# A fused attention and Fourier-mixing kernel: a new order of all its steps, made with a price on changes of the PE array's shape

## The chip, the core and the metric

The kernel runs on one core of a Trainium2 chip. A core has five engines, each with its own in-order queue of instructions: PE (TensorE, matmuls; PEld in the profile is its weight load), DVE (VectorE), ACT (ScalarE), POOL (GpSimd) and SP (SyncE, which here only issues DMAs). The metric is device time in microseconds of one execution.

## The reference

Linear attention with exponential features (8 batches, 8 heads, 576 rows, 64 columns a head, 128 features), whose output goes through a two-dimensional Fourier transform and a two-layer network with a residual. Cut to what matters:

```python
def phi(x):
    proj = x @ w_phi
    proj = proj - max(abs(proj), axis=-1)
    return concatenate([exp(proj), exp(-proj)], axis=-1)
q_p, k_p = phi(q), phi(k)
num = q_p @ (k_p.T @ v)
den = q_p @ sum(k_p, over rows) + 1e-06
x = num / den                              # 8 x 576 x 512
u = x + real(fft(fft(x, axis=1), axis=2))
un = (u - mean(u)) / sqrt(var(u) + 1e-06)
out = u + relu(un @ w_ch1) @ w_ch2         # 512 -> 2048 -> 512
```

## The kernel before

All data of a batch stay on chip; the two network matrices W1b and W2b are loaded once, as bf16. The work of every batch is cut into generators, each with a letter, and each `next` of a generator is one step that emits some instructions:

- K, V, Q issue the loads of a batch's inputs on POOL's DMA queue (`load`, L284); B and A issue the DMA transposes on SP (L408 to L422); W issues the load of W1b (L93) in its first step and of W2b (L95) in its second.
- T makes the features: psk<-wphi,KT for keys and psh, ph for queries on PE, exponentials on ACT. P takes row maxima of the queries (psq on PE, MQ on DVE), R those of the keys (MK on DVE), S scales V by them (V4N, V4P, VCn, VCp on POOL).
- M runs the heads (kv at L887 and L891, pn at L987) and the Fourier stage (pm at L1021, psD at L1045, px at L1075, pu at L1104). D folds rows on DVE, N normalises (UN) and turns it to UT, U makes scales.
- F is the network of a batch: psf<-UT,W1b (L1224), relu to HT on ACT, pso<-W2b,HT (L1241, and L1267 for the last 64 rows).
- Y, C, H, Z, G, J occur in the opening alone: filling matmuls (idle, L1338), constants, sines, pads, and the PE transposes (pst, L368) of batch 0's keys (G) and queries (J).

Batch 0 is treated apart: its K, Q and V are loaded in f32 by SP, on the DMA queue q1 (`load_first`, L336), into space that belongs later to W2b and HT; they are turned on PE. The loads of POOL go through the DMA queue q0. SP's loads have the tiles' names W2b<-in_k_dram, W2b<-in_q_dram, HT<-in_v_dram.

The order of all steps is written out as a string of 1238 letters, `PLAN`; for each letter the kernel takes the next step of that generator. Nothing reorders the instructions afterwards: each engine's queue holds them as they were emitted. How the string came about is not part of the kernel.

A matmul is given a shape of the PE array (rows * columns): 128*128 for most; 64*128 where the contraction is over 64 (psk, psq, psh, ph), two of which use the two halves of the rows; 64*64 for the last 64 rows of keys and queries (L477, L527); 128*64 for the last 64 rows of the output (L1267).

```python
    with tc.manual_schedule():
        count_first()
        load_first()
        count_rest()
        for name in PLAN:
            step(name)
```

Of the kernel before, what the change touches and what calls it, by code (L numbers as in the profile page):

```python
# [20 lines left out]


PLAN = (
    "CCZCYYZYGGCTZVTRZKGTGRZWGJTTSJYRSJTQTTPPYTYRPTJMRJTMSMMSPSTKPTPTZMYTMMQTMTPMCQTMMTMTBDMHKMHKHDDHYAHY"
    "DYMYMHYTMMVMRTQMTNMMYTNTQNNYSFNMFNFNRVRFSTTPTFMFRSYUNTFWMURFVFFFFUUMTPMFBSTFMNTUTPNUSMFVPPCTFMFTUPQM"
    "TFMFTFPATVMFFFMMFTFMFKMFFMQFMFRTKFMFFRFPFDFFFFTFFFFTDFFFDRTFFFMFFTTDMFRFFFFSFFMFFFTFMSMFRFTMTTNMTFMN"
    "FPTMMFSSMTPMFTPPMTFFFMFFQNMPTFBSFMFFQMFFPTFFMNNUAMFFMFMFVTRTFFMFFVRVFFKMFKFFFFTMFMFFFFQMFPFDFFTPFRFF"
    "FTFDPFFTFFDDFFRFFTMFFFTMFFMMBSFFMSFRFTMMTFTNNFMFMMMKFTFMTSTFFFFSMPPTMTFFFFFMFSFMFPTMQQVFFFPTKFFMNNNM"
    "FFMFFMFFUMFFMFMFFFAMTRTVFFRTVFFFFFQMFFFDFDFTFFFDRFTPDFFFTPFFRFFTMFFFFTMMMFSFFRSFTMFTFMTTFNFTFMFNSMMM"
    "FMBSFKTTMQNFFFNPFMTFFFMFTPPFMFSFMNFPQMUTFVFKFPAFFMMFMFFVMFFMTFMFFMFFFMRTFRVFFTFFFQMFFFFTDDFRFFFFTFDP"  # L30
    "FFDFTPFFFRFTMTFFFFFMMMFFRFSFSTMSTFFMTFTFFNMFFTNMMMMSTTFMFFQNFTFPMFFFMFVNFMTBPPFSFMFFTPFMKFFFMFFQPNMF"
    "FMAUKFFMFFFMTTFRFRFMFFFTSFFFFVTMFFFRMTQFFFMTFFFFDFDFFFRFDFTFFDMFTFMFFMFSMFMRFTFFTMFTFTFFTMNNFPSMMMMV"
    "TFFSMTPMSTQFFMTPMFTFBQMFPPPFFMFFMFNVFPFFANNUMFFMFMTFMFFMFFMFFRTFRMFFFFFFFVTTPFSFFRFVFFMTFDFFTFFFDFDR"
    "FFFFFTDMTMFFFFFMMFFSFRFTMFTTTMNFMTNMFFFFMSFMMPSTFMFFFNFPTMFFFFFFMTPPSFMFFMFPTFMFFPNFFTMFNMFFMFMFFUFM"
    "FMFFFFMMFFFFFFMFFFFDFFFDFDFFFDFMFFMFFMFFMMFFMNMFFNFFFFFFMFMFMFFFFFFFFFFFFFFFFFFFNFFFFFNFNFFFUFFFFFFF"
    "FFFFFFFFFFFFFFFFFFFFFFFFFFFFFFFFFFFFFF"
)

# [1368 lines left out]
```

## Time and profile before

| what | value |
|---|---|
| median of 3 runs | 426.52 us |
| the 3 runs | 426.52, 426.04, 428.52 us |
| span of the profiled execution, first to last instruction | 423.1 us |
| its granted TensorE clock | 0.999 |
| DMA: packets, bytes, mean rate | 108761, 42.70 MB, 101 GB/s |

The time of the profiled execution itself is not recorded apart from its span; the median of the runs is 3.4 us above that span. The profile gives, for each engine, the busy time and the number of instructions; the chain of work that ended last, followed back; what each engine waited for; and time lines. A time line merges equal instructions that follow each other (x12) into one row, with its start, its length and, in brackets, the idle time of the engine before it and what ended it. Matmuls overlap, so the distance of two starts tells more than a length.

### The profile page before, as it was taken

What the parts mean: (1) busy time and instruction counts of PE and PEld (TensorE: products, weight loads), DVE (VectorE), ACT (ScalarE), POOL (GpSimd) and SP (SyncE); (2) the same over time, 40 slices, a digit from 0 to 9 for tenths busy, and PEclk for the clock granted to TensorE, in tenths of its full rate; (3) what the DMA queues carried; (4) which work ended last, traced back from release to release, by engine and by line L of the source; (5) the groups of instructions that cost most, each with busy time, mean ns of one, the idle gap of its engine ahead of it and who ended that gap; (6) DMA issues with size and microseconds to landing.
All of it is one profiled execution on the core that took longest, in us unless ns stands there. A gap on an engine that the chain in (4) does not pass through costs nothing.

```text
span 423.1 us, 10390 instructions
## 1 busy us (share of the span) xinstructions
PE 397.4 (94%) x4093; PEld 256.1 (61%) x4122; DVE 331.1 (78%) x681; ACT 306.3 (72%) x626; POOL 207.8 (49%) x271
## 2 busy tenths in 40 slices
PE   8787798999899999999999999999999999999995
PEld 3454475744676558655675558665766567656563
DVE  4989788798979976998779885898989786968103
ACT  6978799748975899489847898588868887353460
POOL 7982688525646077706673282834755331500000
PEclk9999999999999999999999999999999999999999
DMA  8999959984569468853899069954895081103313
GB/s 218 206 165 163 148 88 174 145 83 76 89 102 180 72 101 106 123 84 49 112 153 138 2 91 136 131 71 66 117 138 77 14 102 32 27 0 72 72 26 87
DMA packets 108761, 42.70 MB, mean 101 GB/s; under 512 B 82857, under 2 KB 103721, under 8 KB 108713
## 3 DMA queue, kind: packets, MB, share of 16 engines
q0 software_dynamic: 45936, 16.60, 37.1%
q1 hardware_dynamic: 62215, 24.85, 34.8%
q8 instruction: 32, 0.52, 0.5%
q10 hardware_dynamic: 562, 0.59, 0.5%
q14 instruction: 16, 0.13, 0.1%
HBM read 36.77 MB, written 9.44 MB: 109 GB/s over the span
## 4 chain that ended last, share of the span: by engine, by line
PE 61%; DVE 20%; ACT 8%; POOL 5%; DMA 2%; issue 2%; DVEq 0%; ACTq 0%; POOLq 0%
PE psf L1224 21%; PE pso L1241 19%; DVE R L903 3%; PE kv L887 3%; DVE cb L999 3%; DVE tg L994 2%; PE pso L1267 2%; PE psD L1045 2%; DMA UT<-UN 2%; PE pu L1104 2%; PE psq L547 1%; DVE MK L511 1%; PE psk L491 1%; PE psh L597 1%; DVE X L1094 1%
## 5 line engine op out<-in xcount | busy, mean ns | idle before, releaser
L1224 PE MATMUL psf<-UT,W1b 128*128 128x320 bf16 (+1 forms) x1024 | 142.5, 286 | 2.4 <-DMA UT<-UN 1.5
L1241 PE MATMUL pso<-W2b,HT 128*128 128x512 bf16 x467 | 117.1, 379 | 1.7 <-issue 0.5
L1224 PEld LDWEIGHTS <-W1b 128*128 128x128 bf16 x1024 | 94.0, 98 | 29.7 <-issue 4.3
L1229 ACT ACTIVATE HT<-psf 128x320 bf16<-128x320 f32 x128 | 53.5, 442 | 27.0 <-PE psf L1224 21.6
L1241 PEld LDWEIGHTS <-HT 128*128 128x128 bf16 x496 | 44.8, 98 | 44.6 <-issue 2.6
L1002 POOL TENSOR_TENSOR X<-cb,rd 128x320 f32<-128x320 f32 x56 | 41.5, 746 | 38.6 <-DVE rd L1001 37.3
L466 POOL TENSOR_TENSOR VCn<-VS,VCn 128x512 bf16<-128x512 bf16 x28 | 29.7, 1061 | 38.1 <-ACT VCn L461 35.3
L1231 ACT ACTIVATE HT<-psf 128x512 bf16<-128x512 f32 x64 | 37.9, 605 | 12.6 <-PE psf L1224 12.0
L555 DVE TENSOR_REDUCE MQ<-psq 128x8 f32<-128x1024 f32 (+1 forms) x32 | 34.3, 1084 | 13.4 <-PE psq L547 13.2
L1247 DVE SCALAR_TENSOR_TENSOR X<-pso,rs,X 128x512 f32<-128x512 f32 x31 | 22.8, 735 | 21.6 <-PE pso L1241 21.6
L497 ACT ACTIVATE KPn<-psk 128x1024 bf16<-128x1024 f32 x28 | 28.6, 1021 | 14.0 <-DVE MK L511 13.9
L497 ACT ACTIVATE KPp<-psk 128x1024 bf16<-128x1024 f32 x28 | 28.7, 1025 | 11.1 <-PE psk L491 11.1
L451 POOL TENSOR_TENSOR V4N<-VS,V4N 64x256 bf16<-64x256 bf16 x14 | 8.7, 623 | 53.9 <-ACT V4N L447 53.4
L511 DVE TENSOR_REDUCE MK<-psk 128x8 f32<-128x1024 f32 x28 | 33.9, 1212 | 1.0 <-ACT KPp L497 0.7
L1094 DVE TENSOR_TENSOR X<-pu,X 128x512 f32<-128x512 f32 (+3 forms) x49 | 23.3, 526 | 11.2 <-PE pu L1104 8.9
L466 POOL TENSOR_TENSOR VCp<-VS,VCp 128x512 bf16<-128x512 bf16 x28 | 29.7, 1059 | 0.0
L606 ACT ACTIVATE QPHP<-psh 128x1024 bf16<-128x1024 f32 x28 | 28.9, 1031 | 0.8 <-PE psh L597 0.6
L606 ACT ACTIVATE QPHN<-psh 128x1024 bf16<-128x1024 f32 x28 | 29.0, 1035 | 0.0
L1150 ACT ACTIVATE UN<-X,MV 128x512 bf16<-128x512 f32 (+1 forms) x35 | 24.5, 723 | 5.4 <-DVE MV L1175 3.1
L1174 DVE BATCH_NORM_STATS2 st<-X 128x6 f32<-128x512 f32 (+1 forms) x40 | 27.1, 677 | 0.3
L1190 POOL TENSOR_TENSOR rs<-VE,mhalf 128x5 f32<-128x5 f32 (+1 forms) x9 | 10.3, 1145 | 29.0 <-DVE VE L1189 29.0
L987 PEld LDWEIGHTS <-QPHP 128*128 128x128 bf16 x280 | 21.2, 99 | 4.6 <-DVE cb L999 1.0
(465 smaller groups left out, 825.0 us busy)
## 6 DMA issues: line engine op xcount, KB each, us to landing
out_dram<-X SPq DMA_DIRECT2D x15, 256.0 KB
out_dram<-X SPq DMA_DIRECT2D x60, 64.0 KB
QS<-in_q_dram POOLq DMA_DIRECT2D x14, 256.0 KB, 6.2
KS<-in_k_dram POOLq DMA_DIRECT2D x7, 512.0 KB, 7.4
VS<-in_v_dram POOLq DMA_DIRECT2D x14, 256.0 KB, 5.1
W1b<-in_moe_w_ch_dram POOLq DMA_DIRECT2D x1, 2048.0 KB, 13.1
W2b<-in_moe_w_ch_dram POOLq DMA_DIRECT2D x1, 2048.0 KB, 14.8
W2b<-in_k_dram SPq DMA_DIRECT2D x2, 512.0 KB
```

Of the source, the lines that this page charges most:

```text
L466: nc.gpsimd.tensor_tensor(out=VC[:, hs, :, 0:D], in0=values[b][0][:, hs, :].rearrange("p h (j d) -> p h j d", d=D), in1=VC[:, hs, :, D:D + ...
L497: nc.scalar.activation(out=KP[:, hs, :, :].rearrange("p e (jp jj) f -> p jj (e jp) f", jj=2), in_=psk[:], func=AT.Exp, scale=sgn,)
L511: nc.vector.tensor_reduce(out=MK[:, 2 * pr:2 * pr + 2, :].rearrange("p e (jp jj) -> p jj (e jp)", jj=2), in_=tiles[pr][:], axis=AX.X, op=A ...
L555: nc.vector.tensor_reduce(out=o, in_=i[:], axis=AX.X, op=ALU.max, apply_absolute_value=True)
L606: nc.scalar.activation(out=o, in_=psh[:], func=AT.Exp, scale=sgn)
L1002: nc.gpsimd.tensor_tensor(out=X[:, :, D * h:D * h + D], in0=cb[:, :, 0:D], in1=rd[:].to_broadcast([128, 5, D]), op=ALU.mult,)
L1094: nc.vector.tensor_tensor(out=to, in0=more, in1=to, op=ALU.add)
L1174: nc.vector.bn_stats(out=st[0:M, :], in_=X[0:M, c, 0:C])
L1224: nc.tensor.matmul(ps, lhsT=W1b[:, cc, 128 * hh:128 * hh + 128], rhs=UT[:, cc, lo:hi], start=(cc == 0), stop=(cc == NCC - 1),)
L1229: nc.scalar.activation(out=HT[:, hh, lo:hi], in_=ps, func=AT.Relu, scale=-1.0)
L1231: nc.scalar.activation(out=HT[:, hh - 1:hh + 1, lo:hi], in_=psw[:].rearrange("p (a n) -> p a n", a=2), func=AT.Relu, scale=-1.0,)
L1241: nc.tensor.matmul(po[:], lhsT=HT[:, hh, at:at + 128], rhs=W2b[:, hh, :], start=(hh == 0), stop=(hh == NHH - 1),)
```

## The change

Only the string `PLAN` differs. Every step, and with it every instruction, is the same, 4108 matmuls and all DMAs among them; they stand in another order, in whose making a change of the PE array's shape between successive matmuls was given a price. The first line of 13, of which 12 differ:

```diff
 PLAN = (
-    "CCZCYYZYGGCTZVTRZKGTGRZWGJTTSJYRSJTQTTPPYTYRPTJMRJTMSMMSPSTKPTPTZMYTMMQTMTPMCQTMMTMTBDMHKMHKHDDHYAHY"
+    "WYYYCCGCZZCGTGTGRJTRTTGZJYZSJRTSTPPRYTPYTJRJTSKMMSMTYPMPSTKTPTMMVTMMTTPMMMCTBTMDTHHMMQDHZYYHDDZQYQVA"
...
 )
```

On PE, successive matmuls differ in shape at 205 places before and at 194 now. Taken by stretches: ahead of batch 0's pm 30 and 33, from there to the end 175 and 161. Ahead of the first psf (L1224) stand 472 matmuls before and 500 now; the added ones are 16 psk, 8 psq and 4 pu, while ahead of batch 0's pm there are 400 before and 412 now (4 idle and 8 of L477 more).

POOL in the opening, before. The rows are in the order of its queue: constants, pads, loads into VS, KS and QS for batch 1, the load of W1b, and the multiplications by V of batch 0:

```order
L139 IOTA gs 128x128
L197 TENSOR_SCALAR gs<-ga,pn 128x320 x3
L268 MEMSET QPHP 128x8x64
...
L271 MEMSET V4P 128x520
L284 DMA VS_249<-in_v_dram 64x4x64 x2
L271 MEMSET V4N 128x520
L284 DMA KS_265<-in_k_dram 64x8x64
L274 MEMSET HI_105 128x512
L274 MEMSET HI_106 128x512
L93 DMA W1b<-in_moe_w_ch_dram 128x4x2048
L852 TENSOR_TENSOR V4N<-HT,V4N 64x4x64 x2
```

The same queue now:

```order
L139 IOTA gs 128x128
L93 DMA W1b<-in_moe_w_ch_dram 128x4x2048
L197 TENSOR_SCALAR gs<-ga,pn 128x320 x3
L268 MEMSET QPHP 128x8x64
...
L271 MEMSET V4P 128x520
L271 MEMSET V4N 128x520
L852 TENSOR_TENSOR V4N<-HT,V4N 64x4x64 x2
```

The load of W1b moved ahead of everything that POOL waits for, and the loads of batch 1 moved behind the first multiplications by V.

DVE in the opening, before (L375 copies a transpose of keys, KT, or queries, QT, from PE's results; L838 and L833 are the maxima of the keys; QT_172 is the first piece of Q):

```order
L833 TENSOR_REDUCE MK_180<-ps_236 128x4
L375 CAST KT<-pst 128x512 x2
L838 TENSOR_REDUCE MK<-psk 128x2x4
L375 CAST KT<-pst 128x512
L375 CAST QT_172<-pst 128x2x256
```

And now:

```order
L375 CAST KT<-pst 128x512 x2
L833 TENSOR_REDUCE MK_180<-ps_237 128x4
L375 CAST QT_172<-pst 128x2x256
L838 TENSOR_REDUCE MK<-psk 128x2x4
L375 CAST KT<-pst 128x512
```

The copy of the first piece of Q moved ahead of the maxima of the first pair of heads and of a copy of keys.

PE in batch 3, before (L576 projects the last 64 rows of the queries in shape 64*128, L597 the others; kv is 128*128):

```order
L891 LDWEIGHTS K4n
L891 MATMUL kv<-V4N,K4n 128x65
L576 LDWEIGHTS wphi_97
L576 MATMUL ph_2808<-QT_2211,wphi_97 128x256
...
L1267 LDWEIGHTS HT
L1267 MATMUL pso<-W2b,HT 64x512
```

And now:

```order
L891 LDWEIGHTS K4n
L891 MATMUL kv<-V4N,K4n 128x65
L597 LDWEIGHTS wphi_97
L597 MATMUL psh<-QT_2160,wphi_97 128x512
...
L576 LDWEIGHTS wphi_97
L576 MATMUL ph_2798<-QT_2161,wphi_97 128x256
...
L1241 LDWEIGHTS HT
L1241 MATMUL pso<-W2b,HT 128x512
```

L597 and L576, which have the same shape, stand next to each other now, where L576 stood alone between two other shapes.

More of the change, by code (lines that the diff above doesn't have):

```diff
@@ L23 @@
 PLAN = (
-    "CCZCYYZYGGCTZVTRZKGTGRZWGJTTSJYRSJTQTTPPYTYRPTJMRJTMSMMSPSTKPTPTZMYTMMQTMTPMCQTMMTMTBDMHKMHKHDDHYAHY"
[L25 to L33, printed above, removed]
@@ L34 @@
-    "FFFFFTDMTMFFFFFMMFFSFRFTMFTTTMNFMTNMFFFFMSFMMPSTFMFFFNFPTMFFFFFFMTPPSFMFFMFPTFMFFPNFFTMFNMFFMFMFFUFM"
-    "FMFFFFMMFFFFFFMFFFFDFFFDFDFFFDFMFFMFFMFFMMFFMNMFFNFFFFFFMFMFMFFFFFFFFFFFFFFFFFFFNFFFFFNFNFFFUFFFFFFF"
+    "WYYYCCGCZZCGTGTGRJTRTTGZJYZSJRTSTPPRYTPYTJRJTSKMMSMTYPMPSTKTPTMMVTMMTTPMMMCTBTMDTHHMMQDHZYYHDDZQYQVA"
+    "YVTMMHTMMRTPHSMTTVRMNMMTYQYKNYTNRNSNQMMTFNFTUSNFFFRYFRNMKNWFFMFUUUSTPQMUFTFMTPBFMFFNPCSTFFMTPFMTPUMT"
+    "FFUPTTFAFMFTMFMQFMFMFFMFFPTDFFMRFFFFMFFFRFFKFTDFFTTQDTFDFFFFRFRSVFFFTSMFFMVFTFFFFMMTFSFFMRFSFTMTFMTF"
@@ new lines @@
+    "FNNKPMMMMTMTPMFPQMTPTMFFFFBFNFFSMFTPKMFAFFPTFMNNFMFFMMFUFMTFRTFFFFFRFTMFFMFFMFFMFFTPFQFFQRFFTDFFFTDP"
+    "FFFFDFKDPFFVRMFFTVFFTMVFBFMMKTFSFFMSSFFQTRMFSTFMPNNFMMMFFMTTTFMFFFFTPMTFFFMFFNMFFSVMNFPTMFFAFPTFMNUM"
+    "FFMFMFFFMFFFMMFFFVFFMFTTDFFMFTFFTFFKFRTRFFDFDPRFFDSFFQFVTPFFFFRMMFTTVFTBFFFFSMMFFRFMFTTTMNFTMNMFFMFS"
+    "FMFFMTTMFQFNNQFFSPSMTFFFMFFPTPMFTFMFNFPMAFUFMFPMFMFFMFFVMFFMTTRFQTFMRQFFFSFFFMMFFFTFFDFFFFFRFTFKFDDP"
+    "FFDFTPFRFFFMFFTTFMTFFMFSMFRFSFMFTTTMFFFNFFTMNVKMMMFMFSTTMFFNNFFPMTFSPFFMFFMTPFMFFQMFNPTFBFFPAFFUMMFM"
@@ L36 @@
+    "FFFMTTFMRFKFFVTFFFRMFFQVFFFMTFTFFMFFFMRFFFFFFFTFDFDFFVDFFDFRMFFTTMTFFKMFSMSRFFMFTTTMNMMTNFSFFSFVFFPM"
+    "MMTFFMBTPMFTFMSTPFMTFFMFNPQPPMQFFMFFPNMFFMFFNAFMFMFFFMFUFMTVTFRFTRFFMFFFFFSFPTFFTFFMFFFVFFTFFDFDRFFF"
+    "DRFDFFTTMTMFFFFFFMMSRFFFMFTTTMFNFMMTFSNMFFMFMFSTPFFFFPTMFFFTMNPFNFPPMFFFMFFMFNSFPTFMFTFMFFFMFUMFMFFF"
+    "FMFMFFFMFMFFFFMFFFFFDFFDFDFDFFFMMFFFFMFMFMFFFMNMFNFFFFFMFFMFMFFNFFFFFFFFFFNFFNFFFFFFFFFFUFFFFFFFFFFF"
     "FFFFFFFFFFFFFFFFFFFFFFFFFFFFFFFFFFFFFF"
```

## The prediction

> **What bounds the kernel now.** I read the page first, its busy times and its chain by engine; then the busy time by stretch; then what PE waited for; then single rows of the opening. From the page:
>
> ```profile
> span 423.1 us, 10390 instructions
> PE 397.4 (94%) x4093; PEld 256.1 (61%) x4122; DVE 331.1 (78%) x681; ACT 306.3 (72%) x626; POOL 207.8 (49%) x271
> PE 61%; DVE 20%; ACT 8%; POOL 5%; DMA 2%; issue 2%; DVEq 0%; ACTq 0%; POOLq 0%
> ```
>
> PE is busy 94% of the span and carries 61% of the chain. But the share is a mean over unlike stages, so the span is cut at the matmul pm of batch 0 (41.7 us) and at 80 us (columns: the stretch, its length, then the busy time of PE, PEld, DVE, ACT and POOL with their instructions, the granted clock, the DMA share and GB/s):
>
> ```profile
> 0.00:41.70 41.70, 32.78 (x400) 19.73 (x401) 33.44 (x74) 33.11 (x62) 30.21 (x53) 1.00 1.06 189
> 41.70:80.00 38.30, 32.97 (x403) 22.87 (x403) 30.04 (x75) 34.74 (x74) 27.22 (x36) 1.00 1.12 138
> 80.00:423.10 343.10, 331.64 (x3296) 213.45 (x3321) 267.63 (x534) 238.48 (x492) 150.34 (x183) 1.00 0.65 86
> ```
>
> From 80 us on PE is busy 331.6 of 343.1 us. Before that, nothing is full but the DMA engines (share 1.06 and 1.12); four engines hand work to each other. What PE waited for from 80 us on is little (the largest rows and the smallest; in the view of waits each has total, times and the longest):
>
> ```profile
> PE psf L1224 <- DMA UT<-UN: 1.5, 2, 1.0
> PE ph L576 <- DVE MQ L555: 0.8, 1, 0.8
> PE psf L1224 <- ACT HT L1229: 0.7, 2, 0.3
> ...
> PE psk L491 <- DVE cb L999: 0.2, 1, 0.2
> ```
>
> Its eight rows add up to some 4.6 us. So the last 343 us can gain only what PE itself has less to do, and any delay of the opening goes through to the end.
>
> **The price of a change of shape.** The time line of PE (start, time, instruction; overlapping pieces, so starts are compared):
>
> ```profile
> 201.21 0.19 PE L891 MATMUL kv<-V4P,K4p 128*128 128x65 bf16 x1
> 201.24 0.29 PE L887 MATMUL kv<-VCn,KPn 128*128 128x65 bf16 x4
> 201.37 0.19 PE L891 MATMUL kv<-V4N,K4n 128*128 128x65 bf16 x1
> 201.49 1.49 PE L1267 MATMUL pso<-W2b,HT 128*64 128x512 bf16 x12
> ```
>
> Behind the same matmul L891 the next one of the same shape starts 0.03 us later, and one of shape 128*64 starts 0.12 us later. Nothing is waited for, so the change of shape itself costs 0.09 us. In the order of the instructions PE changes its shape 205 times before and 194 times now; ahead of pm of batch 0 it is 30 and 33, behind it 175 and 161. Behind pm 14 fewer at 0.09 us are worth 1.3 us. Ahead of it the 3 more (0.3 us) lie where PE waits for others, and cost nothing as long as it does.
>
> The Trainium skill, "TensorEngine Tiling (Array Packing)", section Tiling Modes, says that changing the mode, not merely the tile, drains TensorE; the 0.09 us agree. Its page "TensorE: Matmul & The Clock Gate", section Single matmul latency, gives a constant of 166 ns for a matmul that hides no drain; by that figure the same 14 would be an estimated 2.3 us. The row is of this kernel and decides.
>
> **The moved weight load.** The new table begins with W, the step that issues the load of W1b. Before, POOL came to it at 15.7 us (POOL's time line):
>
> ```profile
> 2.92 0.24 POOL L139 IOTA gs<- 128x128 f32 x1
> 4.39 1.57 POOL L197 TENSOR_SCALAR gs<-ga,pn 128x320 f32<-128x320 f32 x3 [1.23 <-DVE pn L192]
> ...
> 15.71 0.79 POOL L93 DMA_DIRECT2D W1b<-in_moe_w_ch_dram  x1
> ```
>
> Now it stands right behind that IOTA, so it is issued at 3.2 us, in a hole of 1.23 us: its 0.79 us on POOL cost nothing. Its transfer is another thing. From 2 to 16 us the DMA engines are full with the first K, Q and V, which SP issues into queue q1. Three windows of the DMA view (queue, packets, MB, share of 16 engines): 5 to 7 us, while K and Q arrive alone; 21 to 26 us, W1b beside a transpose of SP; 76 to 78 us, loads of POOL beside a transpose:
>
> ```profile
> q1 hardware_dynamic: 641, 0.48, 100.0%
> ...
> q0 software_dynamic: 241, 0.99, 97.1%
> q1 hardware_dynamic: 225, 0.06, 8.7%
> ...
> q0 software_dynamic: 572, 0.17, 82.1%
> q1 hardware_dynamic: 571, 0.15, 65.0%
> ```
>
> Two queues that both have work get one packet each in turn, whatever their size: 241 to 225, 572 to 571. W1b's packets carry 4 KB (0.99 MB in 241), so its 2 MB are 512 of them, at 48 per us 10.7 us. While they run, q1 gets through about 512 packets, for which alone it needs 512 / 320 = 1.6 us (641 in 2 us). So everything that q1 holds behind the second piece of K arrives 10.7 - 1.6 = 9.1 us later. That this load was hidden before is due to the transfers ahead of it having ended; that cover is gone. Late next are Q, then V. PE says when Q was needed:
>
> ```profile
> 11.25 0.66 PE L368 MATMUL pst<-ident,W2b 128*128 128x128 f32 x4 [1.06 <-DVE KT L375]
> 12.66 0.63 PE L368 MATMUL pst<-ident,W2b 128*128 128x128 f32 x4 [0.43 <-DMA W2b<-in_q_dram]
> 41.72 0.38 PE L1021 MATMUL pm<-HI,ones_b 128*128 128x512 bf16 x1 [1.81 <-ACT HI L917]
> 53.59 1.04 PE L1224 MATMUL psf<-UT,W1b 128*128 128x256 bf16 x8
> ```
>
> The transposes of the second piece of Q, at 12.66, waited for its DMA, so there was no slack: they go to 21.7 us. What of these 9.1 us reaches pm? From there DVE and ACT are the fuller engines:
>
> ```profile
> 12.30:24.00 11.70, 8.37 (x96) 4.99 (x97) 10.88 (x13) 11.02 (x22) 11.36 (x16) 1.00 1.02 206
> 24.00:31.70 7.70, 7.11 (x129) 5.03 (x129) 6.19 (x13) 5.52 (x17) 6.30 (x9) 1.00 0.94 151
> 31.70:41.70 10.00, 7.74 (x121) 5.03 (x118) 9.40 (x24) 8.03 (x13) 2.42 (x4) 1.00 1.43 164
> ```
>
> DVE works 26.5 of these 29.4 us, so a crowded restart can win back at most 2.9 us; half of that, 1.5, since it waits for PE and ACT, which are as late. DVE has one copy of Q (0.68 us, row below) more behind it at that point than before. That gives pm 9.1 - 1.5 - 0.7 = 6.9 us later; the ends are 9.1 (nothing won back) and 5.5 (all of it).
>
> ```profile
> 13.47 0.68 DVE L375 CAST QT<-pst 128x512 bf16<-128x512 f32 x1
> 14.25 1.23 DVE L838 TENSOR_REDUCE MK<-psk 128x8 f32<-128x1024 f32 x1
> ```
>
> The order would even let DVE lose there: the MK reduction of the first pair (1.23 us), which could run while nothing arrives, now stands behind that copy of Q. This leans to the upper end. The later loads of batch 1, which POOL now issues behind its multiplications, slip with the opening and are not waited for sooner.
>
> **Other work ahead of the first psf.** In the new order 28 matmuls more stand ahead of the first psf of batch 0: 16 psk, 8 psq and 4 pu. At 53.59 us PE had the first psf behind waits:
>
> ```profile
> 46.86 0.54 PE L1075 MATMUL px<-CS,CEO 128*128 128x289 bf16 x3
> 47.74 0.40 PE L491 MATMUL psk<-wphi,KT 64*128 64x128 bf16 x8 [0.35 <-ACT ET L1057]
> 56.88 0.39 PE L547 MATMUL psq<-wphi,QT 64*128 64x128 bf16 x8
> ```
>
> At 0.40 us for eight psk or psq, and as much for the four pu, this is 1.6 us that PE can do in its holes there. The gain lies between 0 (their inputs are late too) and 1.6; I take 1.0, as the holes are there but the keys come from the same late loads.
>
> **The rest of the order.** From pm of batch 1 on the links of each batch (pm, psD, pu, psf) lie within about 2 us of PE work of where they lay. I price that at nothing, with +-1 us: the 4.6 us of waits can shift, but there is little to win or lose.
>
> **Sum.** 6.9 - 1.3 - 1.0 = +4.6 us on the profiled span of 423.1 gives 427.7. The runs have a median of 426.5, 3.4 us above the span; the same 3.4 on top gives 431.1 us. With the ends, 5.5 - 1.3 - 1.6 - 1 = +1.6 and 9.1 - 1.3 + 1 = +8.8: 428.1 to 435.3.
>
> **Rivals.**
> - *The load passes unnoticed.* If q1 kept most of the engines' time while W1b ran, or Q had slack, only the 1.3 us of changes of shape remain: 425.2 us. The even packets speak against it, and the wait at 12.66. For it speaks that q1 there held one transpose at a time, never a deep backlog as in the opening.
> - *Faster.* POOL loses four things ahead of its first multiplication by V (two loads of V, one of K, the issue of W1b, the memsets of HI). If inputs were in time, kv would no longer wait for it (2.1 us in the waits, row below). With 1.3 and 1.6 that makes 421.5 us. It decides only if V lands by about 16 us, as before; by the packets it lands near 25.
>
> ```profile
> PE kv L887 <- POOL VCp L869: 2.1, 3, 1.3
> 16.51 1.34 POOL L852 TENSOR_TENSOR V4N<-HT,V4N 64x256 bf16<-64x256 f32 x2
> ```
>
> - *Nothing is won back and a new wait comes.* The upper end, 9.1 us at pm, with batch 1's loads (behind the late multiplications on POOL) late as well, by the 1 us of the last POOL item: 436 us.
>
> **How the numbers follow.** The forecast gets 0.70, the unnoticed load 0.17, faster 0.07, the last 0.06. The likeliest is 431.1 us. A range of 424.8 to 435.3 takes in the forecast's own 428.1 to 435.3 and the unnoticed load at 425.2, and leaves out about 0.15. About 1% (4.3 us) is what a measurement of this kernel can tell from no change: under 422.3 is faster, over 430.8 slower. The forecast lies at that border: 0.6 of its 0.70 is above it, with the last rival 0.48 slower. Faster is 0.06, since part of that rival stays within 1%. The rest, 0.46, is the same.
>
> **What would show it.** W1b's issue near 3.2 us on POOL, and 4 KB packets between 5 and 16 us. The transposes of Q at 20 to 22 us, waiting for the DMA of Q; V4N on POOL at 22 us or later; pm of batch 0 at 47 to 51 us instead of 41.7; from pm on to the end 1 to 4 us less than the 381.4 us of before. I am wrong if Q's transposes stand near 12.7 us (queues do not share so), or if pm is late but the time is not (the later stages had slack that the waits do not show), or if waits of psf for UT grow beyond 1.5 us.

## The result and the profile after

The changed kernel takes 451.3 us (median of 4 runs, 450.05 to 455.71), the kernel before 426.28 us beside it: a ratio of 1.061 (1.055 to 1.067). It is 25 us slower. I had forecast 431.1 us and a range up to 435.3.

The page of the changed kernel, first its span, its busy times, the granted clock by slices and the chain by engine:

```profile
span 449.4 us, 10389 instructions
PE 405.8 (90%) x4093; PEld 261.5 (58%) x4122; DVE 329.8 (73%) x681; ACT 306.3 (68%) x626; POOL 208.7 (46%) x271
...
PEclk9599769979999999999999996999999999999998
...
PE 64%; DVE 14%; DMA 11%; ACT 6%; issue 2%; POOL 1%; SPq 0%; DVEq 0%; POOLq 0%; ACTq 0%
```

The span grew by 26.3 us. PE does the same matmuls and is busy 8.4 us longer (405.8 against 397.4), and idle for the other 17.9 us. DMA has 11% of the chain, where it had 2%. The clock line has digits below 9 in five places; before, it was 9 in every slice (mean 0.999).

The stretches of the changed kernel, cut at the same work as before (pm of batch 0 starts at 48.9 us now), and below them four that are cut where the granted clock changes. The columns are those of the windows in the prediction:

```profile
0.00:48.90 48.90, 35.40 (x412) 21.46 (x413) 30.01 (x74) 33.23 (x63) 33.45 (x60) 0.90 0.87 151
48.90:87.20 38.30, 32.94 (x337) 21.31 (x338) 27.84 (x67) 31.87 (x66) 20.64 (x25) 0.82 0.92 114
...
13.40:23.60 10.20, 3.47 (x21) 2.91 (x22) 2.34 (x3) 1.80 (x2) 0.00 (x0) 0.50 1.10 244
50.90:64.50 13.60, 10.14 (x60) 5.13 (x61) 9.27 (x23) 8.39 (x18) 5.37 (x8) 0.50 0.94 106
95.30:102.10 6.80, 4.40 (x37) 2.81 (x38) 3.34 (x6) 1.90 (x3) 3.12 (x4) 0.50 0.54 63
272.80:279.60 6.80, 3.02 (x21) 2.27 (x22) 0.44 (x1) 0.60 (x1) 1.68 (x3) 0.50 1.08 123
```

In the second stretch PE starts 337 matmuls in 38.3 us; in the same length after its pm the kernel before started 403. In the last four the granted clock is 0.50: PE runs at half speed.

What PE waits for, ahead of 41 us (first row) and from there on:

```profile
PE pst L368 <- DMA W2b<-in_q_dram: 10.4, 1, 10.4
...
PE psf L1224 <- DMA UT<-UN: 8.8, 3, 5.7
PE psq L547 <- DMA QT<-QS: 5.1, 2, 2.7
PE psk L491 <- DVE cb L999: 3.5, 4, 2.4
```

So there is one long wait in the opening, for Q, and then single waits of 2 to 6 us in the later stages, for transposes by DMA (QT, UT) above all, and for DVE. Put against the same work in the trace of before, the delay grows in steps (the 65th psf of a batch stands for the middle of its network):

| work | before, us | now, us | delay | forecast of the delay |
|---|---|---|---|---|
| pm of batch 0 | 41.7 | 48.9 | +7.2 | +6.9 |
| first psf of batch 0 | 53.6 | 67.4 | +13.8 | +5.9 |
| 65th psf of batch 0 | 69.9 | 80.8 | +10.9 | |
| pm of batch 1 | 93.5 | 112.0 | +18.5 | |
| pm of batch 4 | 235.7 | 255.0 | +19.4 | |
| 65th psf of batch 4 | 272.4 | 299.2 | +26.8 | |
| end | 423.1 | 449.4 | +26.3 | +4.6 |

The first row is as forecast. The rest is not: three jumps, of 6.6 us between pm and the first psf of batch 0, of 7.6 us by pm of batch 1, and of 7.4 us in batch 4.

**The first jump.** PE's time line of the changed kernel:

```profile
20.13 1.09 PE L368 MATMUL pst<-ident,W2b 128*128 128x128 f32 x4 [10.37 <-DMA W2b<-in_q_dram]
...
48.90 0.39 PE L1021 MATMUL pm<-HI,ones_b 128*128 128x512 bf16 x1 [0.44 <-ACT HI L917]
51.13 0.61 PE L491 MATMUL psk<-wphi,KT 64*128 64x128 bf16 x8 [1.84 <-DVE CEO L1034]
...
55.96 0.61 PE L547 MATMUL psq<-wphi,QT 64*128 64x128 bf16 x8 [2.66 <-DMA QT<-QS]
56.50 1.63 PE L1045 MATMUL psD<-CS,CEO 128*128 128x289 bf16 x6
57.92 0.93 PE L1075 MATMUL px<-CS,CEO 128*128 128x289 bf16 x3
```

The eight psq of batch 1, which stood behind the first psf before (at 56.88), now stand ahead of the last psD and of px. PE takes its work in order, so the Fourier stage of batch 0 waits behind them for QT of batch 1. And all of it runs at half clock: three px take 0.93 us here and took 0.54 before. Of the 6.6 us, 4.4 are longer busy time of PE (from pm to the first psf 13.44 us for 88 matmuls, at a mean granted clock of 0.63, against 9.06 for 72); the rest is idle time. QT is late since its transposes are. SP's time line, the first transpose of these queries, before:

```profile
39.52 1.25 SPq L420 DMA_TRANSPOSE QT<-QS  x1
```

and now:

```profile
47.73 4.71 SPq L420 DMA_TRANSPOSE QT<-QS  x1
```

It takes 4.7 us instead of 1.25. The DMA view (queue, packets, MB, share of 16 engines) shows what runs beside it. From 39 to 44 us in the kernel before:

```profile
q1 hardware_dynamic: 3710, 0.92, 90.0%
q0 software_dynamic: 36, 0.02, 5.2%
```

and from 47 to 56 us in the changed one:

```profile
q1 hardware_dynamic: 3573, 0.89, 76.8%
q0 software_dynamic: 1086, 0.53, 73.5%
```

About as many packets of q1 needed 9 us instead of 5; POOL's loads of K, V and Q, issued between 36 and 45 us, run beside them.

**The second jump.** Between the middle of batch 0's network and pm of batch 1, PE waits twice, first for QT of batch 2 and then for DVE:

```profile
95.35 0.61 PE L547 MATMUL psq<-wphi,QT 64*128 64x128 bf16 x8 [2.40 <-DMA QT<-QS]
98.31 0.61 PE L491 MATMUL psk<-wphi,KT 64*128 64x128 bf16 x8 [2.35 <-DVE cb L999]
```

With the half clock from 95.3 to 102.1 us PE is also busy 3.2 us longer there (26.18 against 22.99, for 259 matmuls against 251), so waits and clock make up the 7.6 us.

**The last jump.** In batch 4, POOL (first two rows) issues a load of V and one of K, 768 KB, as SP begins the transposes of UT that psf needs:

```profile
264.11 0.81 POOL L284 DMA_DIRECT2D VS<-in_v_dram  x1
264.91 0.90 POOL L284 DMA_DIRECT2D KS<-in_k_dram  x1
...
266.80 2.81 SPq L1167 DMA_TRANSPOSE UT<-UN  x2
...
270.57 3.82 SPq L1167 DMA_TRANSPOSE UT<-UN  x2
...
276.58 2.74 PE L1224 MATMUL psf<-UT,W1b 128*128 128x256 bf16 x12 [5.69 <-DMA UT<-UN]
```

The DMA view of 265 to 272 us:

```profile
q0 software_dynamic: 1530, 0.77, 88.7%
q1 hardware_dynamic: 449, 0.36, 23.2%
```

The load gets 1530 packets through and the transposes with the stores 449. The wait is 5.7 us, and the twelve psf behind it take 2.74 us at half clock. In the kernel before the same twelve, at 252.41 us, took 1.48 us and had waited 0.47 us.

### The profile page after: what moved, and what is told of

It reads as the page before. It is cut to its first block, busy times and chain, and to the rows that moved or that the text cites. A ratio compares the mean times of both kernels' runs of the same rounds, so it can differ in the third digit from the quotient of the medians.

```text
span 449.4 us, 10389 instructions
## 1 busy us (share of the span) xinstructions
PE 405.8 (90%) x4093; PEld 261.5 (58%) x4122; DVE 329.8 (73%) x681; ACT 306.3 (68%) x626; POOL 208.7 (46%) x271
## 4 chain that ended last, share of the span: by engine, by line
PE 64%; DVE 14%; DMA 11%; ACT 6%; issue 2%; POOL 1%; SPq 0%; DVEq 0%; POOLq 0%; ACTq 0%
PE psf L1224 23%; PE pso L1241 17%; DMA W2b<-in_q_dram 4%; DMA QT<-QS 4%; PE kv L887 3%; DMA UT<-UN 3%; DVE cb L999 3%; PE psD L1045 3%; DVE tg L994 2%; PE psk L491 2%; PE pu L1104 2%; PE pso L1267 2%; DVE R L903 2%; PE psq L547 1%; PE idle L1338 1%
## 5 line engine op out<-in xcount | busy, mean ns | idle before, releaser
L1224 PE MATMUL psf<-UT,W1b 128*128 128x320 bf16 (+1 forms) x1024 | 144.4, 289 | 9.5 <-DMA UT<-UN 8.8
L1224 PEld LDWEIGHTS <-W1b 128*128 128x128 bf16 x1024 | 95.4, 99 | 37.7 <-DMA UT<-UN 9.1
L1229 ACT ACTIVATE HT<-psf 128x320 bf16<-128x320 f32 x128 | 53.6, 446 | 29.3 <-PE psf L1224 23.0
L1002 POOL TENSOR_TENSOR X<-cb,rd 128x320 f32<-128x320 f32 x56 | 41.7, 747 | 57.0 <-DVE rd L1001 42.0
L606 ACT ACTIVATE QPHN<-psh 128x1024 bf16<-128x1024 f32 x28 | 28.9, 1031 | 0.0
L284 POOL DMA_DIRECT2D QS<-in_q_dram x28 | 23.4, 837 | 5.0 <-DMA QT<-QS 4.9
```

What stands on the lines that cost most here:

```text
L606: nc.scalar.activation(out=o, in_=psh[:], func=AT.Exp, scale=sgn)
L1002: nc.gpsimd.tensor_tensor(out=X[:, :, D * h:D * h + D], in0=cb[:, :, 0:D], in1=rd[:].to_broadcast([128, 5, D]), op=ALU.mult,)
L1224: nc.tensor.matmul(ps, lhsT=W1b[:, cc, 128 * hh:128 * hh + 128], rhs=UT[:, cc, lo:hi], start=(cc == 0), stop=(cc == NCC - 1),)
L1229: nc.scalar.activation(out=HT[:, hh, lo:hi], in_=ps, func=AT.Relu, scale=-1.0)
```

## The experiments

PLAN's edits are written with the steps spelled out: K6.1 is the second step of generator K for batch 6. Of each only the moved steps stand there with a neighbour. The kernel before had medians of 425.6 to 426.0 us beside these runs; each ratio is to that.

| run | what it is | median, us | ratio |
|---|---|---|---|
| e1 | before, W1b's load first | 436.26 | 1.025 (1.021 to 1.029) |
| e2 | changed, W1b's load back | 443.80 | 1.041 (1.038 to 1.044) |
| e3 | old opening, new rest | 438.95 | 1.031 (1.027 to 1.036) |
| e4 | new opening, old rest | 437.33 | 1.026 (1.023 to 1.029) |
| e5 | e3 with two loads earlier | 432.20 | 1.014 (1.011 to 1.016) |
| e6 | old order for 77 steps more, new rest | 450.56 | 1.058 (1.054 to 1.063) |
| e8 | e1 with idle matmuls in the gap | 436.09 | 1.024 (1.021 to 1.028) |
| e9 | before, ten changes of shape fewer | 431.11 | 1.012 (1.010 to 1.015) |
| e10 | changed, all loads at their old places | 449.55 | 1.057 (1.053 to 1.061) |
| e11 | e10, SP's transposes of keys and queries too | 449.53 | 1.056 (1.054 to 1.059) |
| e12 | e2 with two steps of psq back | 441.09 | 1.034 (1.028 to 1.039) |
| e13 | e12 with four loads earlier | 434.74 | 1.021 (1.017 to 1.025) |

None is faster than the kernel before.

**e1: the early load of W1b alone.** The kernel before with one letter moved:

```diff
-    "CCZCYYZYGGCTZVTRZKGTGRZWGJTTSJYRSJTQTTPPYTYRPTJMRJTMSMMSPSTKPTPTZMYTMMQTMTPMCQTMMTMTBDMHKMHKHDDHYAHY"
+    "WCCZCYYZYGGCTZVTRZKGTGRZGJTTSJYRSJTQTTPPYTYRPTJMRJTMSMMSPSTKPTPTZMYTMMQTMTPMCQTMMTMTBDMHKMHKHDDHYAHY"
...
```

> The kernel before with one letter moved: the first W, the load of W1b, stands at the front. Theory A (the early load explains the whole loss: Q late by 10 us, PE idle, clock halved, everything behind it disturbed): Q's transposes at about 22 us, pm of batch 0 at 48 to 50 us, and 446 to 452 us in all. Theory B (the early load costs the opening alone, the rest of the loss is waits for DMA that the new order makes by itself): the same Q and pm, but 433 to 438 us. Theory C (queues do not share, the wait for Q came from elsewhere): Q at 12.7 us and 426 us.

It cost 10.6 us by the medians. The profiled execution is the slowest of the four, 2.5 us above the median. In it PE waits 12.0 us for Q by DMA, 10.9 the longest; pm of batch 0 starts at 54.2 us, 12.5 later, and the same 12.5 us later stand the first psf of batch 0 and pm of batches 1 and 2; the delay ends at 13.8 us. So an opening that is late goes through to the end, and a load put ahead of the first inputs makes it late, both as forecast. 12.5 us is more than the 7.2 us of the changed kernel; part of that is the new order of the opening, which by itself puts pm 2.6 us earlier (e2, next).

**e2: the changed kernel with W1b's load back**, right ahead of POOL's first multiplication by V:

```diff
-W0.0 Y0.0 Y0.1
+Y0.0 Y0.1
...
-Z0.3 S0.0
+Z0.3 W0.0 S0.0
```

> The changed kernel with one letter moved back: the first W stands right ahead of the first S, where W1b is issued behind the first K, Q and V. Theory A: Q's transposes wait less than 1 us, no stretch at half clock in the opening, and 424 to 427 us in all. Theory B: the opening is as before (pm at 41 to 43 us), but waits of psq for QT and of psf for UT remain, and it takes 436 to 444 us. Theory C: no gain, 450 us.

It wins only 7.5 of the 25 us. The wait for Q is gone and pm of batch 0 stands at 39.1 us, 2.6 earlier than in the kernel before; even so the kernel is 17.5 us slower. Its waits:

```profile
PE psf L1224 <- DMA UT<-UN: 9.7, 4, 5.5
PE psq L547 <- DMA QT<-QS: 5.4, 2, 2.8
PE psk L491 <- DVE cb L999: 3.5, 4, 2.4
```

These are the same waits as in the changed kernel. They are not a consequence of the late opening but belong to the new order. So do the jumps: against before, e2 is 2.6 us early at pm of batch 0, 3.6 late at the first psf, 8.6 at pm of batch 1 and 21.8 at the 65th psf of batch 4.

**e3 and e4: the halves of the order.** e3 keeps the order of before up to the first step of N of batch 0 (117 steps) and then takes what is left in the new order; e4 does the opposite with 120 steps of the new one:

```diff
-PLAN = (new order)
+PLAN = (old order up to N0.0) + (the other steps, in the new order)
```

> The steps up to the first N of batch 0 in the order of before, all others in the new order. Theory A: 424 to 427 us, by the changes of shape saved (1.3 us) rather below before. Theory B: waits for QT and UT in the new order remain, 434 to 442 us. If the price of the changes of shape is a gain anywhere, it is here.

> The steps up to the first N of batch 0 in the new order (W1b at the front), all others in the order of before. Theory A: 446 to 452 us. Theory B: 433 to 438 us; then this and the kernel with the old opening add up to the loss of the changed one.

e3 loses 13.3 us and e4 11.7; the 25.1 us together are as much as the whole loss of the changed kernel. By this cut about half goes with the opening and half with the order behind it.

**e5: two loads moved in e3.** The largest wait of e3 is again psf for UT in batch 4. The last load of V for batch 5 and the second of K for batch 6 (256 and 512 KB) are put right behind the load ahead of them, some 18 to 30 us earlier:

```diff
-V5.1 M4.11
+V5.1 V5.2 M4.11
...
-K6.0 F3.39
+K6.0 K6.1 F3.39
...
-N4.1 V5.2 K6.1 M4.23
+N4.1 M4.23
```

> The kernel with the old opening and the new order behind it (439 us), with two steps moved: the load of the second half of V of batch 5 (256 KB) and of K of batch 6 (512 KB), which run beside the transposes of UT of batch 4, stand right behind the loads that precede them on POOL, some 18 to 30 us earlier. Theory L (loads beside the transposes make PE wait there): the wait of psf for UT of 5.4 us falls under 1.5 us, the stretch at half clock behind it is gone, and 430 to 433 us in all. Theory S (SP's stores, or UN itself, are late): the wait stays over 4 us and the time at 438 to 440 us.

6.8 us less. PE's row and the DMA view of 256 to 262 us in e3:

```profile
265.30 2.74 PE L1224 MATMUL psf<-UT,W1b 128*128 128x256 bf16 x12 [5.42 <-DMA UT<-UN]
...
q0 software_dynamic: 1505, 0.75, 95.2%
q1 hardware_dynamic: 1112, 0.46, 64.7%
```

and in e5:

```profile
258.67 1.48 PE L1224 MATMUL psf<-UT,W1b 128*128 128x256 bf16 x12 [1.08 <-DMA UT<-UN]
...
q1 hardware_dynamic: 1381, 0.57, 68.8%
q0 software_dynamic: 767, 0.05, 24.3%
```

The wait falls from 5.4 to 1.1 us and the twelve matmuls from 2.74 to 1.48 us. Only the two loads moved, so this shows what the last jump is: loads beside SP's transposes, and the half clock behind the wait.

**e6: another cut.** As e3, but the old order is kept for 194 steps:

```diff
-PLAN = (old order up to N0.0) + (the other steps, in the new order)
+PLAN = (old order up to F0.16) + (the other steps, in the new order)
```

> As the kernel with the old opening (439 us), but the order of before reaches 74 steps further, to the 17th step of the network of batch 0. In the kernel with the old opening, psk, psq and pu between 47 and 60 us wait for each other's inputs, and the clock is halved from 52.4 to 59.2 us. If that is a loss of the new order there (theory L as well as S), 435 to 437 us; if the 3.3 us are lost to something before the cut, 439 us.

A miss: more of the old order, and 11.6 us slower than e3. It waits 12.9 us in all for UT, the longest 5.8. The cut is itself a change: what the new order had done by then comes later and beside other transfers. So the halves of e3 and e4 hold for their cut alone, and do not tell which steps belong together.

**e8: idle matmuls in the gap.** e1 with twelve steps of Y (48 idle matmuls) more ahead of the first transposes of Q:

```diff
-WCCZCYYZYGGCTZVTRZKGTGRZGJTTSJ
+WCCZCYYZYGGCTZVTRZKGTGRZGYYYYYYYYYYYYJTTSJ
...
-        for i in range(15):
+        for i in range(27):
```

> The kernel with W1b's load at the front (436 us, 20 us at half clock behind a wait of 11 us), with 48 idle matmuls more, 10.4 us of them, ahead of the transposes of Q, so that PE is busy while Q is late. Theory H (the halved clock holds up what follows the wait): no half clock in the opening, pm of batch 0 at 50 to 52 us instead of 54.2, and 432 to 434 us. Theory N (DVE, ACT and POOL set the pace there): pm at 54 us, 435 to 437 us.

The idle time is filled, and the clock stays. From 12.6 to 33.2 us, in e1:

```profile
12.60:33.20 20.60, 10.10 (x64) 5.46 (x64) 6.33 (x9) 7.80 (x14) 10.52 (x15) 0.50 0.87 170
```

and with the idle matmuls:

```profile
12.60:33.20 20.60, 18.05 (x130) 8.57 (x129) 7.83 (x11) 8.15 (x16) 9.22 (x14) 1.00 0.78 161
```

pm of batch 0 comes 1.7 us earlier (52.5 against 54.2), but the medians are 436.09 and 436.26 us, and the ratios 1.024 and 1.025, which is no difference. What the half clock costs in that opening stays open, though, since the idle matmuls also run past the arrival of Q: its first transposes start at 23.60 us here and at 21.26 in e1. From them to pm it is 28.9 us here and 32.9 in e1, where PE waited another 1.1 us for Q; so in these two profiles the full clock won time, and the later start took part of it back.

**e9: fewer changes of shape alone.** The kernel before with six steps moved by at most three steps of PE each, so that like shapes follow each other: ten changes fewer behind pm of batch 0, nearly as many as the change made (14), and no load, store or transpose moved against another. Three of the six:

```diff
-F1.33 P3.0 F1.34 D2.0 F1.35 F1.36 T3.3
+F1.33 F1.34 D2.0 F1.35 F1.36 P3.0 T3.3
...
-D2.1 P3.2 F1.42 F1.43 T3.5
+D2.1 F1.42 F1.43 P3.2 T3.5
...
-D4.2 P5.0 F3.40 F3.41 D4.3 F3.42 T5.5
+D4.2 F3.40 F3.41 D4.3 F3.42 P5.0 T5.5
```

> The kernel before with six steps (one step of row maxima or of features each) moved by at most three steps of PE, so that matmuls of one shape stand together: 10 changes of shape fewer, no load, store or transpose moved against another. If a change costs PE 0.095 us and PE is the bound there: 0.95 us less, 424.5 to 425.2 us. If moving the steps costs as much in waits: 425 to 427 us. Over 428 us: even this little is enough to disturb the order.

A miss, and the sign is the other: 5.1 us slower. The first row of its waits, and where the first of them lies on PE and on DVE:

```profile
PE psq L547 <- DVE MQ L555: 3.9, 3, 1.7
...
136.52 0.40 PE L547 MATMUL psq<-wphi,QT 64*128 64x128 bf16 x8 [1.69 <-DVE MQ L555]
...
135.26 1.21 DVE L555 TENSOR_REDUCE MQ<-psq 128x8 f32<-128x1024 f32 x1
```

A maximum of 1.2 us on DVE has to clear each eight psq, which take 0.4 us on PE. Put next to other feature work, the second psq comes before DVE has cleared its place. Ten changes of shape by the 0.09 us of the prediction are 0.9 us, an estimate; the waits of 3.9 us took that back several times over. They are most of the 5.1 us; where the rest lies is open.

**e10 and e11: all loads back.** The changed order with every step of W, K, V and Q where it stood before, counted in the other steps ahead of it, and in e11 A and B too. For the sake of the buffers, the multiplications by V of batches 1, 6 and 7 (S) stand up to one step of S later than in the changed order, and the first loads of V for batches 1 and 2 wait for the multiplications of the batch ahead. The start of e10, in the steps of W, K, V, Q, A, B and S alone:

```diff
-W0.0 S0.0 S0.1 S0.2 K1.0 S0.3 S0.4 K1.1 V1.0 B1.0 Q1.0 Q1.1 Q1.2 V1.1 A1.0 V1.2 S1.0
+K1.0 W0.0 S0.0 S0.1 Q1.0 S0.2 S0.3 S0.4 V1.0 K1.1 Q1.1 Q1.2 B1.0 K2.0 K2.1 A1.0 V1.1 Q2.0 Q2.1 S1.0 V1.2
...
```

> The changed order with the load steps of all batches (W, K, V and Q, all on POOL's queue q0) put back to where they stood before, counted in the other steps ahead of them; the transposes of SP and all work of PE, DVE and ACT stay in the new order. Theory L (the new order loses by where its loads lie against the transposes on SP's queue, and by the halved clock behind each wait): of the 17.5 us that the changed order with W1b alone put back still lost, most goes: 428 to 434 us, no wait of psf for UT above 2.5 us, at most two halved stretches. Theory C (the order of PE's, DVE's and ACT's work itself costs that time, wherever the loads lie): 440 to 446 us, the waits for QT and UT as long as with W1b alone put back (2.6, 2.8, 5.5 us).

> As the kernel with all loads put back, and the steps that issue SP's transposes of keys and queries (A, B) put back as well. Theory L: 426 to 433 us, not slower than the kernel with the loads alone. Theory C: 440 to 446 us. A third, M (both halves: DMA waits go, but PE's work of like shapes comes closer together than DVE clears it, as in the kernel with ten fewer changes of shape): 432 to 438 us in both, with waits of psk and psq for DVE of 1 to 3 us left and UT waits below 2 us.

Both miss. Two rows of the waits of e10:

```profile
PE kv L887 <- POOL VCp L466: 6.6, 4, 3.1
PE psf L1224 <- DMA UT<-UN: 4.0, 5, 1.7
```

The long waits for UT fall as expected (from 5.5 us to 1.7) and those of L547 for QT are gone, but the kernel is 5.8 us slower than e2: now kv waits for POOL, whose multiplications by V stand behind their loads and behind loads that wait for their buffers. The old places of the loads belong to the old order. How much of this the later multiplications add was not tried apart.

**e12 and e13: the named waits, one kind after the other.** e12 is e2 with the two steps of psq put back that made PE wait for QT:

```diff
-T1.2 P1.0 H0.5
+T1.2 H0.5
...
-F0.3 F0.4
+F0.3 P1.0 F0.4
...
-F0.28 P2.0 T2.1
+F0.28 T2.1
...
-F0.33 F0.34
+F0.33 P2.0 F0.34
```

e13 moves four loads as well, each right behind the load ahead of it:

```diff
-K4.1 D2.3 ... F1.57 Q4.2 T3.9
+K4.1 Q4.2 D2.3 ... F1.57 T3.9
...
-Q5.0 F2.42 ... F2.64 Q5.1 F2.65
+Q5.0 Q5.1 F2.42 ... F2.64 F2.65
...
-V5.1 M4.11 ... K6.0 F3.39 ... N4.1 V5.2 K6.1 M4.23
+V5.1 V5.2 M4.11 ... K6.0 K6.1 F3.39 ... N4.1 M4.23
```

> The changed order with W1b's load put back to its place ahead of POOL's first multiplication by V, and with two more steps put back to about where they stood before: the eight psq of batch 1 that stand ahead of px (behind the fourth step of psf again) and the eight psq of batch 2 at 85 us (six steps of psf later). No load or transpose moves. Theory Q (PE, which takes its work in order, stands behind matmuls whose QT is not there yet, and then runs at half clock): the waits of 2.6 and 2.8 us for QT go, with the wait for DVE of 2.4 us at 88.5 and the halved stretch at 85.4 us: 433 to 439 us instead of 443.8. Rival (the transposes set the end: whoever needs QT next waits as long): 442 to 445 us, with waits for QT a few us later.

> As the kernel with the two steps of psq put back, and four loads on POOL's queue moved away from SP's transposes of UT: the second of K for batch 6, the last of V for batch 5, the last of Q for batch 4 and the middle of Q for batch 5 stand 20 to 120 steps earlier, right behind the load ahead of them. Theory L: the waits of psf for UT of 1.9, 2.1 and 5.5 us shrink below 1.2 us each and the halved stretches behind them go; 8 to 13 us less than the kernel with the steps of psq alone: 424 to 430 us. Rival (the moved loads collide with what lies beside their new places, or POOL's issue delays its multiplications): less than 4 us gained, with new waits for QT, KT or VCp.

e12 takes 2.7 us off e2, less than the 5 to 11 expected, and the intervals of the two ratios overlap a little, so the gain is hardly clear of noise: the waits for QT are gone, but pn waits 2.1 us for DVE at 84.6 us instead. e13 takes off another 6.4, again less than the 8 to 13 expected. In the two profiles pm of batch 1, which lies ahead of the first load that moved, already stands at 99.4 us in e12 and at 97.3 in e13, so up to 2.1 us of the 6.4 may not be the loads'. What is left to wait for in e13:

```profile
PE psf L1224 <- DMA UT<-UN: 3.1, 2, 2.0
PE pn__1639 L987 <- DVE cb L999: 2.7, 1, 2.7
PE psf L1224 <- DVE MQ L555: 2.5, 2, 1.7
```

The 5.5 us in batch 4 are down to 1.0 (its first twelve psf now at 261.6 us), while the UT of batch 3 still comes 2.0 us late. The ladder by the medians: 451.3 as changed, 443.8 with W1b back, 441.1 with the psq back, 434.7 with the four loads moved, 425.9 before. Seven steps out of 1238, moved for when inputs arrive and what runs beside them, carry 16.6 of the 25 us. The last 8.8 us lie in many waits of 1 to 3 us and in half clock; which steps they belong to is open. Most of them lie in the stretch of the first two jumps: from pm of batch 0 to pm of batch 1 it is 51.8 us in the kernel before, 63.1 in the changed one and still 58.7 in e13, with 516 to 518 matmuls in each. So e5 and e13 show the cause of the last jump, and that of the first two is shown only in part.

## Why the prediction was wrong

**The opening was right in its mechanism, and near in its size by luck.** W1b's load is issued at 3.11 us (forecast 3.2). From 9 to 16 us the queues take turns, packet by packet (DMA view of the changed kernel):

```profile
q0 software_dynamic: 331, 1.36, 95.2%
q1 hardware_dynamic: 327, 0.16, 11.6%
```

Q's transposes come at 20.13 us (forecast 20 to 22), V4N at 24.48 us (22 or later), pm of batch 0 7.2 us late (6.9). e1 shows that a delay there is not won back later. The parts of the 6.9 came out otherwise, as e2 shows, which is the same order without the early load. Q's first transposes stand at 11.06 us in e2, so the load makes them 9.1 us late, as forecast. At pm that has become 9.8 us (48.9 against 39.1): nothing is won back, where I took off 1.5. And the new order by itself brings pm 2.6 us forward, where I counted 0.7.

The Trainium skill, "DMA: Bandwidth & Descriptors", section Queues, rings and completion order, says that an engine alternates between the queues it has work for, a packet at a time; the 331 to 327 agree. In batch 4 of the changed kernel it was 1530 to 449, so the turns were not even there, perhaps because q1 did not always have a packet ready; no run tells.

**"Other work ahead of the first psf" had the wrong sign.** I took 28 matmuls more ahead of the first psf for a gain of 1.0 us. The way from pm to the first psf became 6.6 us longer; 2.9 us of that come back by the 65th psf, as work done early need not be done later. Putting the eight psq back, with those of batch 2, won 2.7 us in all (e12), so they are a part of it. I had asked whether PE had holes for these matmuls, and had not asked for each of them when its input is there and what stands behind it. The eight psq waited 2.7 us with psD, px, pu and psf behind them. The sentence that the loads of batch 1 "are not waited for sooner" was wrong for the same step: the psq that needs them moved ahead, while the transposes became slower.

**"The rest of the order", priced "at nothing, with +-1 us", was the step that failed.** It cost some 12 to 13 us: 26.3 at the end less the 13.8 at the first psf, and 13.3 in e3, where the opening is that of before. Of the 12.5, 4.7 us arise between the first psf of batch 0 and pm of batch 1, where my sum had no term at all, and 7.8 from there on. The argument was that the links of each batch lie within 2 us of PE work of where they lay. That says nothing on what the other queues do at that moment. Loads moved far against SP's transposes: the last of V for batch 5 stands 37 steps of F later than before and the second of K for batch 6 stands 52 later, right beside the transposes of UT of batch 4. Moving these two back ahead won 6.8 us in e5. The transposes had next to no slack, as the 1.5 us of waits for UT before should have told me: a wait that ends at a DMA is slack of zero, not a small sum. The condition under which I would be wrong, "if waits of psf for UT grow beyond 1.5 us", is the one that came true, at 8.8 us.

**No term for the granted clock.** With 0.999 throughout, the trace of before gave no cause to think of it. Of the 26.3 us, the 8.4 us of longer busy time of PE fit this: the matmuls are the same. What it costs depends on the stage. In the opening e8 leaves it open; behind the late UT it is 1.3 us on twelve matmuls (2.74 against 1.48).

**The price of a change of shape.** The 1.3 us for 14 changes can't be seen under 26 us, and no run measured them apart. The 0.09 us of one change holds where the next matmul is a pso in both cases: behind L891 at 200.08 us the pso of shape 128*128 starts 0.03 us later, and the one of 128*64 in the prediction 0.12 us later. e9 shows that they need not come at no cost: with ten changes fewer, the kernel before lost 5.1 us, with 3.9 us of new waits for DVE.

**The rivals.** None was near. The late rival, 436 us, looked for its new wait in the opening; the waits that came were spread over batches 0 to 4.

## What to carry to other kernels

When an order is changed as a whole, price it queue by queue: for each load that moves, look at which transposes or stores run at its new place, and for each matmul that moves ahead, at when its input arrives and at what stands behind it. A wait for a DMA that is small but not zero marks a place without slack. A cost that the search for an order adds (here a price on changes of shape) is worth having only if the search also prices the waits that its savings bring.

## What the runs showed of the hardware

A PE that idles loses half its clock, and the loss outlasts the idle time. In the changed kernel PE stood idle from 9.8 to 20.1 us; the granted clock was 0.50 from 13.4 to 23.6. The stretches at 0.50 lasted 10.2, 13.6, 6.8 and 6.8 us in the rows above, near multiples of 3.4 us. A wait of 5.7 us was followed by 3.0 us more at half clock, up to 279.6. Idle matmuls in the gap held the clock at 1.00 (e8).

The Trainium skill, "TensorE: Matmul & The Clock Gate", section HAM oscillation — how this bites in real kernels, gives as the rule that PE should have no idle gaps above some 3.4 us. The lengths agree with such a window. But the stretch from 50.9 us began in a wait of 1.84 us, the only one above 0.5 us in the 3.4 us ahead of it. The 3.4 us ahead of the last three stretches of the changed kernel:

```profile
47.50:50.90 3.40, 1.29 (x12) 0.44 (x9) 3.33 (x10) 2.73 (x5) 2.10 (x4) 1.00 1.83 142
91.87:95.28 3.41, 1.08 (x8) 0.55 (x6) 1.01 (x3) 1.03 (x3) 0.00 (x0) 1.00 1.44 174
269.37:272.78 3.41, 1.52 (x26) 0.79 (x22) 3.27 (x7) 2.98 (x6) 3.41 (x4) 1.00 1.35 192
```

PE was busy for 1.29, 1.08 and 1.52 us of these, in several pieces. So it need not be one long gap; a window in which PE is idle for the greater part was enough here. In the other runs it is the same: ahead of each such stretch PE was busy for at most 1.7 of 3.4 us.

A transpose by DMA can take several times as long while a load runs beside it: 4.7 us instead of 1.25 for the same transpose of queries. For that one the load is named as the cause from the packets beside it alone; for those of UT, e5 moved the loads and the wait went.
